# Three of the first loads asked for by ScalarE, the decay factors as a planned step, and a re-planned start

## The chip, the cores and the metric

One NeuronCore of one Trainium2 chip runs the whole kernel. The metric is the device time of one execution in microseconds; the kernel before took 299.38 us (median of three runs, 299.16 to 300.62).

## What is computed

A retention layer (attention without a softmax, with a decay by distance) feeds a feed-forward layer with an ELU. Eight batches, eight heads, 576 positions, head size 64; the feed-forward goes from 512 to 2048 and back to 512, over 8 x 576 = 4608 tokens.

```
scores = (q @ k^T) / 8                                   # per batch and head
D[i, j] = gamma_h ** (i - j)  where i >= j, else 0       # gamma_h = 1 - 2 ** (-5 - h)
x = ((scores * D) @ v)  -> [4608, 512]
h = x @ w_in                                             # [512, 2048]
g = where(h > 0, h, exp(min(h, 0)) - 1)
out = g @ w_out                                          # [2048, 512], float32
```

## The kernel before

**Tiling.** A sequence of 576 is cut in chunks of 64. The decay is split into a factor on the queries and one on the keys, `gq` and `gk` (lines 299 to 315: a table load on ScalarE and two exponentials), so that a chunk needs a triangular mask, and everything earlier goes through a running state, the sum of scaled keys times values. An *item* is one batch and 256 positions (or the last 64 of four batches, X and Y). The items of batches 0 and 1 are further cut by heads into two *units* of four heads each, numbered 0 to 7; units 0 and 1 make item 0, units 2 and 3 item 1. A unit goes through these steps: load q and k into one tile (`r`, `rqk`) and v into another, shared by the item's two units; scale the even and the odd positions of q and k by the factors (line 548, tile `st`, four halves, VectorE or GpSimd); cast v (line 558, tile `vn`); transpose q and k on TensorE (line 580) and copy them out of PSUM (line 586, tile `T`), or from unit 5 on transpose by DMA (line 569); scores and their mask (line 914, tile `pt`); its state (matmuls `f<-vn,st`), summed by VectorE (`mid`, lines 849 and 851) and cast (`s`, line 867); and the output of the unit, state part and value part, copied to `xt` (line 950).

**Feed-forward.** A block is 256 tokens (blocks 0 and 1 are items 0 and 1). `ffn1` multiplies `xt` by pieces of `w_in` into one PSUM bank at a time (`f<-xt,w_in_sb`), ScalarE and VectorE make the ELU of it (lines 1067 to 1091, tile `g`), and `ffn2` multiplies by `w_out` (`f<-w_out_sb,g`, 128x512). Block 0's `ffn1` needs the outputs of units 0 and 1 in `xt`.

**What sets the order.** Every step is an `Op` with a cost on each engine that may run it, the steps it depends on, the buffers it takes and a rank. `Plan.run` (lines 67 to 198) goes through time by these costs and gives, engine by engine, the step of lowest rank that is ready; its order is what is emitted, and each engine then runs in that order and waits on semaphores. A planned time is not seen by the chip, the order alone is. `AT` (line 227) holds a named step back to a planned time, `RANKS` (line 228) shifts its rank, `LEAD` and `ULEAD` set how far attention runs ahead of the feed-forward, `EARLY` how many units go through `early` (line 1026: scores, state and output apart) instead of `stretch` (line 998: a unit's output together with the next one's scores), and `UAPART` after which units a stretch is closed by itself. Where the plan leaves TensorE idle in the first 50 us, fillers on a zero tile are put in (lines 1213 to 1223).

**Loads.** All loads of q, k and v are issued by SyncE (line 389), chained in one order (`chain[0]`, line 412): q and k of units 0 and 1, then v of both, then units 2 and 3 alike. The weights are cast on the way by GpSimd's DMA queue, `w_in` in five pieces (line 480) and `w_out` in four (line 491). `HOLD` (line 225) puts a one-column copy on GpSimd (line 400) that reads a piece of a weight and writes the tile of a load, so that the load is asked for only when that piece has landed: unit 4's queries behind the second piece of `w_out` (`wo1`).

Of the kernel before, what the change touches and what calls it, by code (L numbers as in the profile page):

```python
# [11 lines left out]
FP32 = mybir.dt.float32  # L12
# [23 lines left out]
class Plan:  # L36
# [6 lines left out]
    def add(self, *a, **kw):  # L43
        op = Op(*a, **kw)
        self.ops.append(op)
        for key in op.use:
            self.users.setdefault(key, []).append(op)
            op.turn += self.owner.get(key, [])
        for cls, key, *_ in op.take:
            self.owner[key] = [op]  # L50
            if cls not in FREE:
                op.turn += self.takers.get(cls, [])
                self.takers[cls] = [op]
        return op
# [151 lines left out]
ISSUE = 0.65  # L206
# [2 lines left out]
TWO, STEP = 2, 4  # L209
WI, WI1, LD = 1.3, 1.65, 0.84  # L210
MOST, MOSTU = 4, 3
BD_POOL = 0.46
UB_POOL = 0.33
SCALED = 1.06
OUT = "SP"

LEAD = 128
LATE = 26.0
ULEAD = 80
UB = 2  # L220
EARLY = 6
PE_TURN = 5
APART = ()
UAPART = (7,)
HOLD = {"ldq4": "wo1"}
VLATE = (0, 1)
AT = {"wi0": 8.5, "wi1": 10.7, "wi2": 9.0, "wi3": 11.8, "wi4": 14.4, "wo0": 17.4, "wo1": 17.7, "wo2": 19.9, "wo3": 25.3, "so_0_0_0_0": 74, "so_0_1_0_0": 74, "so_1_0_0_0": 74, "so_1_1_0_0": 74, "so_2_0_0_0": 76, "so_2_1_0_0": 76, "ub2_0": 15.33, "md_4_2": 89.01, "F2_3_1_0_0": 78.57, "st2": 14.97, "g_2_6": 63.17, "cq1_0_4": 59.08, "T0_0": 4.92, "us7_1": 60.01, "F2_0_1_12_0": 46.64, "md_3_3": 66.87, "md_1_7": 35.82, "us5_0": 44.11, "ex_2_4": 55.85, "ex_2_2": 53.67, "xc1_u4": 43.93}
RANKS = {"us1_0": -2, "F1_0_1": 4, "mask0_7": 2, "g_2_1": -2, "md_3_3": 8, "A7": -4, "cv1_5": -4}
FREE = ("f", "e", "em", "g", "ot")
SURE = 3  # L230
ATT = ((0, 0), (0, 1), (1, 0), (1, 1), (2, 0), (2, 1), (3, 0), (3, 1), (4, 0), (4, 1), "X",
# [12 lines left out]
def kernel(  # L244
# [9 lines left out]
    nc = tc.nc  # L254
# [18 lines left out]
    pin = tc.keep_in_program_order  # L273
# [38 lines left out]

    (gq, gk), product, powers = decay("", pos, 4)
    product(nc.vector)
    powers()
    pos2_i = const.tile([P, 7], I32, name="pos2_i")
    pos2 = const.tile([P, 7], FP32, name="pos2")
    (gq2, gk2), product2, powers2 = decay("2", pos2, 7)
# [12 lines left out]
    plan = Plan(SLOTS)  # L331
    add = plan.add
# [4 lines left out]
    def T(cls, key, shape, dt):  # L337
        return (cls, key, shape, dt)
# [8 lines left out]
    for n, key in enumerate(ATT):  # L347
        it = Work()
# [6 lines left out]
        if not it.tail and it.b < UB:  # L355
            for w in range(2):
                u = Work()
# [25 lines left out]
    chain, holds = {}, []  # L383
# [2 lines left out]

    def load_part(name, dst, src, key, first, shape, cost=(0.9, 32)):
        def emit(op):
            pin(nc.sync.dma_start(dst(), src))  # L389

        hold = None
        if first and name in HOLD:
            behind = HOLD[name]

            def emit_h(op):
                one = tiles[key][:, 0, :1]
                if isinstance(behind, str):
                    i = int(behind[2:])
                    mark = w_in_sb[:, 0, 256 * W_IN[i][0] :] if behind[1] == "i" else w_out_sb[:, 4 * W_OUT[i][0]]
                    pin(copy[op.eng](one, mark[:, :1]))  # L400
                else:
                    pin(alu[op.eng].memset(one, 0.0))

            hold = add(f"hold{name}", {"POOL": 0.1}, [], emit_h, len(plan.ops) - 1000, take=[T("r", key, shape, FP32)])
            if isinstance(behind, str):
                holds.append((hold, behind))
            else:
                hold.early = behind
            first = False
        op = add(name, {"SP": ISSUE}, [hold], emit, len(plan.ops), take=[T("r", key, shape, FP32)] if first else [],  # L410
                 use=[] if first else [key], dma=cost, after=chain.get(0))
        if not name[3:].isdigit():
            op.most = MOST
        elif int(name[3:]) >= 5:
            op.most = MOSTU
        chain[0] = op
        return op

    def runs(src, b, hs, T):
        return src[b, hs, TB * T : TB * (T + 1), :].rearrange("h (p e) d -> p h (e d)", e=2)  # L420

    def load(it):
        n = it.n
        shape = [P, 2 * H, D]
        if it.units:
            for u, what in [(u, what) for u in it.units for what in "qkv"] if it.n not in VLATE else \
                    [(u, what) for u in it.units for what in "qk"] + [(u, "v") for u in it.units]:
                hs = slice(4 * u.w, 4 * u.w + 4)
                if what == "q":
                    u.ld = {}  # L430
                if what == "v":
                    u.ld["v"] = load_part(
                        f"ldv{u.n}", lambda hs=hs: tiles["rv", n].rearrange("p (h e) d -> p h (e d)", e=2)[:, hs],
                        runs(v, it.b, hs, it.T), ("rv", n), u.w == 0, shape, (LD, 32))
                    continue
                i = "qk".index(what)
                u.ld[what] = load_part(
                    f"ld{what}{u.n}",
                    lambda u=u, i=i: tiles["rqk", u.n].rearrange("p (h e) d -> p h (e d)", e=2)[:, 4 * i : 4 * i + 4],
                    runs((q, k)[i], it.b, hs, it.T), ("rqk", u.n), i == 0, shape, (LD if u.n or not i else 1.4, 32))  # L440
            return
        it.ld = {}
        for name, src in (("v", v), ("k", k), ("q", q)):
            key = ("r" + name, n)
            it.ld[name] = []

            def part(tag, lo, n, s, b, t, key=key, src=src, name=name):
                def dst():
                    if s is None:
                        return tiles[key][lo : lo + n].rearrange("p (h e) d -> p h (e d)", e=2)  # L450
                    return tiles[key][lo : lo + n, s * H : (s + 1) * H]

                def rows_in():
                    if s is None:
                        return src[b, :, t : t + 2 * n, :].rearrange("h (p e) d -> p h (e d)", e=2)
                    return src[b, :, t : t + n, :].rearrange("h p d -> p h d")

                it.ld[name].append(load_part(f"ld{name}{tag}_{it.n}", dst, rows_in(), key, not it.ld[name], shape,
                                             ((1.8 if s is None else KV) * n / P, 64 * n // P)))

            if not it.tail:
                t = TB * it.T
                for s in (None,) if name == "q" else range(2):
                    part("" if s is None else s, 0, P, s, it.b, t + P * (s or 0))
            elif name == "q":
                for c in range(NC):
                    part(c, c * R, R, None, it.b + c, 2 * TB)
            else:
                for s in range(2):
                    for par in range(2):  # L470
                        part(2 * s + par, par * C, C, s, it.b + 2 * s + par, 2 * TB)
# [65 lines left out]
    def prepare_unit(u):  # L537
        n = u.n
        key, vkey, tkey = ("qkn", n), ("vn", n), ("qkT", n)
        hs, begun, cq = slice(4 * u.w, 4 * u.w + 4), {}, {}  # L540
        for i in range(2):
            for e in range(2):
                g = (gq, gk)[i][:, 2 * u.T + e, hs].rearrange("p (x y) -> p x y", y=2)
                g = g.unsqueeze(3).to_broadcast([P, 2, 2, D])

                def emit(op, i=i, e=e, g=g):
                    raw = tiles["rqk", n].rearrange("p (h e) d -> p h e d", e=2)[:, 4 * i : 4 * i + 4, e]
                    pin(alu[op.eng].tensor_tensor(tiles[key][:, i, e].rearrange("p (y x) d -> p x y d", y=2),  # L548
                                                  raw.rearrange("p (x y) d -> p x y d", y=2), g, ALU.mult))

                kw, use = taking(begun, "st", key, [P, 2, 2, 4, D])
                cq[i, e] = add(f"c{'qk'[i]}{e}{n}", {"POOL": 0.62, "DVE": 0.5} if n < 4 else {"POOL": 0.64, "DVE": (0.6, 1.5)},
                               [u.ld["qk"[i]]], emit, u.rank, use=[("rqk", n), *use], **kw)
                begun.setdefault(key, cq[i, e])
        u.ck = [cq[1, 0], cq[1, 1]]

# [10 lines left out]
        if n >= PE_TURN:  # L567
            def emit_t(op):
# [3 lines left out]
                            use=[key], dma=(1.7, 64))]  # L572
            return
        u.turned = []
        for i in range(2):
            bkey = ("T", n, i)

            def emit_t(op, i=i, bkey=bkey):
                for j in range(4):
# [3 lines left out]
                    use=[key])  # L583
# [4 lines left out]
            kw, use = taking(begun, "T", tkey, [P, 8, P])  # L588
# [553 lines left out]

    for it in items:
        load(it)
    tables = late_tables()
    for it in order_of:
        (prepare_unit if it.unit else prepare_item)(it)
# [28 lines left out]
    for blk in blocks:  # L1176
        base, n = (blk.at + len(blk.its)) * 16 + 1, blk.w // P
# [20 lines left out]
    for name, shift in RANKS.items():  # L1198
        if name in named:
            named[name].rank += shift  # L1200
    order = plan.run({"PE": 1.3, "DVE": 2.2, "ACT": 3.0, "POOL": 4.4, "SP": 0.8})
    if PRINT:
        PRINT(order)
        return
# [54 lines left out]
```

## Time and profile before

| | |
|---|---|
| median of the runs | 299.38 us (299.16 to 300.62) |
| profiled execution | 299.8 us |
| its span, first to last instruction | 298.1 us |
| granted TensorE clock | 1.0 |
| TensorE busy | 288.0 us, 97% |
| VectorE, ScalarE, GpSimd busy | 66%, 56%, 40% |
| DMA | 50.67 MB, mean 170 GB/s |

How to read the rows: a timeline row is start, length in us, engine, line, operation, what is written and read, how many in a row, and in brackets how long the engine stood idle before it and what ended that. PE is TensorE, DVE VectorE, ACT ScalarE, POOL GpSimd, SPq the queue of SyncE. PE's matmuls overlap, so that the length of a group runs to the end of its last one, past the start of the next group. A row of stretches is its bounds and length, the busy time with the number of instructions, the granted clock, the DMA engines' busy share, and GB/s.

### The profile page before, as it was taken

The numbers are of one execution on the slowest core, as the hardware profiler recorded it, in microseconds if no ns is written. First come the engines' busy times: TensorE is split into PE (matmuls) and PEld (weight loads), VectorE is DVE, ScalarE is ACT, GpSimd is POOL, SyncE is SP. The second block draws the span as 40 slices with busy tenths as digits, with TensorE's granted clock in tenths as the row PEclk, the third lists the DMA queues.
The fourth block names the chain that finished last, engine by engine and source line by source line (L and its number), as shares of the span: only waits on it lengthen the run. The fifth ranks groups of instructions, "written<-read, shape, count | busy, mean of one in ns | idle before, by whom it ended". The sixth has DMA issues, their size and how long they took to land.

```text
span 298.1 us, 9218 instructions
## 1 busy us (share of the span) xinstructions
PE 288.0 (97%) x3821; PEld 188.0 (63%) x3859; DVE 196.8 (66%) x368; ACT 166.0 (56%) x306; POOL 118.2 (40%) x187
## 2 busy tenths in 40 slices
PE   6999999999999999999999999999999999999995
PEld 3778545866585857685866676767766444444444
DVE  4969633976577738878778666786786477766500
ACT  3779514855276737565656365766665568644311
POOL 5970097762536708263574462916550000000000
PEclk9999999999999999999999999999999999999999
DMA  7999999999899997989886999995761100011221
GB/s 206 286 204 207 238 272 203 256 194 243 281 189 234 195 240 206 158 227 237 196 218 143 251 215 244 177 232 128 178 107 39 73 0 35 2 36 35 50 93 70
DMA packets 128618, 50.67 MB, mean 170 GB/s; under 512 B 92608, under 2 KB 124096, under 8 KB 128576
## 3 DMA queue, kind: packets, MB, share of 16 engines
q1 hardware_dynamic: 123824, 45.89, 66.0%
q0 software_dynamic: 4752, 4.19, 8.8%
q8 instruction: 30, 0.49, 0.7%
q14 instruction: 12, 0.10, 0.1%
HBM read 36.70 MB, written 9.44 MB: 155 GB/s over the span
## 4 chain that ended last, share of the span: by engine, by line
PE 85%; DMA 8%; POOL 2%; issue 2%; SPq 1%; DVE 0%; ACT 0%; POOLq 0%; ACTq 0%
PE f L276 85%; DMA w_out_sb<-in_moe_w_out_dram 5%; DMA r<-in_q_dram 2%; DMA r<-in_v_dram 2%; POOL st L548 1%; SPq L389 1%; POOL w_in_sb L480 1%; PE f L580 0%; POOL w_out_sb L491 0%; POOL s L867 0%; POOL vn L558 0%; ACT ot L1128 0%; DVE mid L851 0%; POOL r L400 0%; DVE pt L914 0%
## 5 line engine op out<-in xcount | busy, mean ns | idle before, releaser
L276 PE MATMUL f<-xt,w_in_sb 128*128 128x256 bf16 (+1 forms) x1022 | 135.9, 286 | 0.4 <-DMA w_in_sb<-in_moe_w_in_dram 0.3
L276 PE MATMUL f<-w_out_sb,g 128*128 128x512 bf16 (+1 forms) x556 | 131.3, 373 | 3.2 <-issue 2.1
L276 PEld LDWEIGHTS <-w_in_sb 128*128 128x128 bf16 x1024 | 99.5, 98 | 33.7 <-DMA w_in_sb<-in_moe_w_in_dram 0.4
L1067 ACT ACTIVATE e<-f 128x512 f32<-128x512 f32 x144 | 85.5, 598 | 58.0 <-PE f L276 55.1
L276 PEld LDWEIGHTS <-g 128*128 128x128 bf16 x592 | 56.4, 98 | 54.8
L1081 DVE TENSOR_SCALAR em<-e 128x512 bf16<-128x512 f32 x75 | 41.2, 555 | 33.8 <-ACT e L1067 33.6
L1089 DVE SCALAR_TENSOR_TENSOR g<-e,f 128x512 bf16<-128x512 f32 x69 | 46.1, 683 | 11.6 <-ACT f L1077 10.7
L1091 DVE SCALAR_TENSOR_TENSOR g<-f,em 128x512 bf16<-128x512 f32 x75 | 50.6, 687 | 4.1 <-DVE em L1081 0.5
L605 POOL CAST kv<-r 128x512 bf16<-128x512 f32 x27 | 16.2, 613 | 56.5 <-issue 27.5
L950 ACT CAST xt<-f 128x512 bf16<-128x512 f32 (+1 forms) x37 | 21.8, 643 | 29.5 <-PE f L276 29.3
L1077 ACT ACTIVATE f<-f 128x512 f32<-128x512 f32 x64 | 37.7, 595 | 0.0
L1128 ACT COPY ot<-f 128x512 f32<-128x512 f32 (+1 forms) x37 | 21.4, 578 | 24.4 <-PE f L276 24.2
L625 POOL TENSOR_TENSOR kv<-r,gq 128x512 bf16<-128x512 f32 x28 | 30.5, 1107 | 10.4 <-DMA r<-in_q_dram 10.4
L625 POOL TENSOR_TENSOR kv<-r,gk 128x512 bf16<-128x512 f32 x28 | 29.5, 1062 | 3.8 <-DMA r<-in_k_dram 3.8
L918 DVE TENSOR_TENSOR pt<-f,mask 128x512 bf16<-128x512 f32 x28 | 18.0, 684 | 8.7 <-PE f L276 8.7
L903 POOL CAST bd<-S 128x256 bf16<-128x256 f32 x40 | 15.3, 405 | 13.0 <-DVE S L891 6.5
L891 DVE TENSOR_TENSOR S<-f,S 128x256 f32<-128x256 f32 x36 | 15.2, 422 | 7.2 <-PE f L276 4.7
L914 DVE TENSOR_TENSOR pt<-f,mask_u 128x512 bf16<-128x512 f32 x16 | 10.3, 685 | 3.0 <-PE f L276 3.0
L276 PEld LDWEIGHTS <-kv 64*64 64x64 bf16 x832 | 11.2, 104 | 0.1
L276 PE MATMUL f<-T 64*64 64x64 bf16 (+1 forms) x576 | 9.6, 199 | 0.0
L548 POOL TENSOR_TENSOR st<-r,gk 128x256 bf16<-128x256 f32 x12 | 8.0, 681 | 1.8 <-DMA r<-in_k_dram 1.8
L548 POOL TENSOR_TENSOR st<-r,gq 128x256 bf16<-128x256 f32 x10 | 6.2, 635 | 6.4 <-DMA r<-in_q_dram 6.4
(66 smaller groups left out, 128.5 us busy)
## 6 DMA issues: line engine op xcount, KB each, us to landing
r<-in_k_dram SPq DMA_DIRECT2D x32, 256.0 KB, 4.5
r<-in_v_dram SPq DMA_DIRECT2D x32, 256.0 KB, 4.7
out_dram<-ot SPq DMA_DIRECT2D x31, 256.0 KB, 2.9
r<-in_q_dram SPq DMA_DIRECT2D x12, 512.0 KB, 5.3
r<-in_q_dram SPq DMA_DIRECT2D x8, 256.0 KB, 4.4
w_out_sb<-in_moe_w_out_dram POOLq DMA_DIRECT2D x4, 512.0 KB, 14.4
w_in_sb<-in_moe_w_in_dram POOLq DMA_DIRECT2D x3, 512.0 KB, 9.7
out_dram<-ot SPq DMA_DIRECT2D x10, 128.0 KB, 2.3
```

The source lines that it names most:

```text
L276: return pin(nc.tensor.matmul(*a, **kw))
L548: pin(alu[op.eng].tensor_tensor(tiles[key][:, i, e].rearrange("p (y x) d -> p x y d", y=2), raw.rearrange("p (x y) d -> p x y d", y=2), g, ...
L605: pin(copy[op.eng](heads(tiles[nkey][:, VS[s]]), tiles["rv", n][:, s * H : (s + 1) * H]))
L625: pin(alu[op.eng].tensor_tensor(tiles[nkey][:, 2 * i + j].rearrange("p (y x d) -> p x y d", y=2, x=HP), raw.rearrange("p (x y) d -> p x y ...
L918: pin(nc.vector.tensor_tensor(pt.rearrange("p h s n -> p (h s) n"), src.rearrange("p (h n) -> p h n", n=C), mask.rearrange("p e r -> p (e ...
L950: pin(copy[op.eng](dst, src))
L1067: pin(nc.scalar.activation(tiles[ekey], tiles[hkey], AF.Exp))
L1077: pin(nc.scalar.activation(ph, ph, AF.Relu))
L1081: pin(alu[op.eng].tensor_scalar_add(em, e, -1.0))
L1089: pin(nc.vector.scalar_tensor_tensor(g, e, -1.0, ph, ALU.add, ALU.min))
L1091: pin(nc.vector.scalar_tensor_tensor(g, ph, 0.0, tiles[mkey], ALU.max, ALU.min))
L1128: pin(copy[op.eng](tiles[okey][:, :width], tiles[pkey][:, :width]))
```

## The change

Three loads, the keys of unit 0 and the values of units 0 and 1, are issued by ScalarE on its own queue and leave the chain of SyncE's loads. The two exponentials that make `gq` and `gk` become a planned step on ScalarE behind the first of these loads, and the scaling of q and k depends on it. The planner's start for ScalarE goes from 3.0 to 0.8 with it. Unit 4's queries are held behind the first piece of `w_out` instead of the second, and unit 6's behind the third (no hold before); the last piece of `w_out` is held back to a planned 34.4 instead of 25.3, and the first pieces of `w_in` move to 8.0 to 8.6. Unit 5 leaves the early ones and closes its stretch by itself; LEAD and most held times and ranks are new.

```
+ASKED = ("ldk0", "ldv0", "ldv1")
-LEAD = 128
+LEAD = 144
-EARLY = 6
+EARLY = 5
-UAPART = (7,)
-HOLD = {"ldq4": "wo1"}
+UAPART = (5, 7)
+HOLD = {"ldq4": "wo0", "ldq6": "wo2"}
...
-AT = {"wi0": 8.5, "wi1": 10.7, "wi2": 9.0, "wi3": 11.8, "wi4": 14.4, "wo0": 17.4, "wo1": 17.7, "wo2": 19.9, "wo3": 25.3,
...
+AT = {"wi0": 8.0, "wi1": 8.6, "wi2": 8.5, "wi3": 12.6, "wi4": 14.4, "wo0": 17.4, "wo1": 17.4, "wo2": 20.5, "wo3": 34.4,
...
     product(nc.vector)
-    powers()
...
-            pin(nc.sync.dma_start(dst(), src))
+            pin((nc.scalar if op.eng == "ACT" else nc.sync).dma_start(dst(), src))
...
+        own = name in ASKED
+        op = add(name, {"ACT" if own else "SP": ISSUE}, [hold], emit, -10 ** 5 if name == ASKED[0] else len(plan.ops), take=[T("r", key, shape, FP32)] if first else [],
+                 use=[] if first else [key], dma=cost, after=None if own and first else chain.get(0))
...
-        chain[0] = op
+        if not own:
+            chain[0] = op
...
-                    runs((q, k)[i], it.b, hs, it.T), ("rqk", u.n), i == 0, shape, (LD if u.n or not i else 1.4, 32))
+                    runs((q, k)[i], it.b, hs, it.T), ("rqk", u.n), i == 0, shape, (LD, 32))
...
-                               [u.ld["qk"[i]]], emit, u.rank, use=[("rqk", n), *use], **kw)
+                               [u.ld["qk"[i]], factors], emit, u.rank, use=[("rqk", n), *use], **kw)
...
+    factors = add("factors", {"ACT": 1.9}, [], lambda op: powers(pin), -10 ** 4,
+                  after=next((op for op in plan.ops if op.name in ASKED), None))
...
-    order = plan.run({"PE": 1.3, "DVE": 2.2, "ACT": 3.0, "POOL": 4.4, "SP": 0.8})
+    order = plan.run({"PE": 1.3, "DVE": 2.2, "ACT": 0.8, "POOL": 4.4, "SP": 0.8})
```

In the built program SyncE's first loads become q0, q1, k1, q2, k2, q3, k3, v2, v3, and ScalarE's stream begins with k0, the table load, `gq`, `gk`, v0, v1, the cast of v0, the copy of unit 1's transposed keys, a `mid`, the cast of v1. GpSimd scales halves of all four of the first q and k tiles, asks for three pieces of `w_in` in a row, and casts only the values of unit 3 of the first four. VectorE casts the first `s` before it scales unit 2. On TensorE the state of unit 0 stands before the scores of unit 1, and the states of units 2 and 3 stand behind the first matmuls with `w_in`.

More of the change, by code (lines that the diff above doesn't have):

```diff
@@ L220 @@
 UB = 2
-EARLY = 6
+EARLY = 5
 PE_TURN = 5
 APART = ()
-UAPART = (7,)
-HOLD = {"ldq4": "wo1"}
+UAPART = (5, 7)
+HOLD = {"ldq4": "wo0", "ldq6": "wo2"}
 VLATE = (0, 1)
-AT = {"wi0": 8.5, "wi1": 10.7, "wi2": 9.0, "wi3": 11.8, "wi4": 14.4, "wo0": 17.4, "wo1": 17.7, "wo2": 19.9, "wo3": 25.3, "so_0_0_0_0": 74, "so_0_1_0_0": 74, "so_1_0_0_0": 74, "so_1_1_0_0": 74, "so_2_0_0_0": 76, "so_2_1_0_0": 76, "ub2_0": 15.33, "md_4_2": 89.01, "F2_3_1_0_0": 78.57, "st2": 14.97, "g_2_6": 63.17, "cq1_0_4": 59.08, "T0_0": 4.92, "us7_1": 60.01, "F2_0_1_12_0": 46.64, "md_3_3": 66.87, "md_1_7": 35.82, "us5_0": 44.11, "ex_2_4": 55.85, "ex_2_2": 53.67, "xc1_u4": 43.93}
-RANKS = {"us1_0": -2, "F1_0_1": 4, "mask0_7": 2, "g_2_1": -2, "md_3_3": 8, "A7": -4, "cv1_5": -4}
+AT = {"wi0": 8.0, "wi1": 8.6, "wi2": 8.5, "wi3": 12.6, "wi4": 14.4, "wo0": 17.4, "wo1": 17.4, "wo2": 20.5, "wo3": 34.4, "so_0_0_0_0": 74, "so_0_1_0_0": 74, "so_1_0_0_0": 74, "so_1_1_0_0": 74, "so_2_0_0_0": 76, "so_2_1_0_0": 81.47, "F2_3_1_0_0": 81.39, "st2": 14.97, "g_2_6": 63.17, "cq1_0_4": 59.08, "us7_1": 60.01, "F2_0_1_12_0": 46.64, "md_3_3": 66.87, "md_1_7": 35.82, "us5_0": 44.11, "ex_2_4": 55.85, "ex_2_2": 53.67, "xc1_u4": 43.93, "ex_4_3": 87.58, "xc0_4": 82.16, "A7": 54.89, "g_1_3": 27.7, "ex_1_2": 24.95, "md_4_3": 88.96, "F1_4_0": 84.27, "bd2_3": 77.5, "cq12": 11.22, "F2_3_0_8_0": 78.02, "ex_2_0": 51.62, "ck17": 46.4, "g_6_3": 120.63, "cv7": 47.86, "cv1_4": 50.56, "us2_1": 17.29, "us0_1": 11.57}
+RANKS = {"us1_0": -2, "F1_0_1": 4, "mask0_7": 2, "g_2_1": -2, "md_3_3": 8, "A7": -4, "cv1_5": -4, "cv1_6": 4, "mask1_u6": 8, "F1_1_1": -4, "so_5_0_0_0": -8, "md_4_1": 2, "F1_1_0": 8}
 FREE = ("f", "e", "em", "g", "ot")
@@ L409, in load_part @@
             first = False
-        op = add(name, {"SP": ISSUE}, [hold], emit, len(plan.ops), take=[T("r", key, shape, FP32)] if first else [],
-                 use=[] if first else [key], dma=cost, after=chain.get(0))
+        own = name in ASKED
+        op = add(name, {"ACT" if own else "SP": ISSUE}, [hold], emit, -10 ** 5 if name == ASKED[0] else len(plan.ops), take=[T("r", key, shape, FP32)] if first else [],
+                 use=[] if first else [key], dma=cost, after=None if own and first else chain.get(0))
         if not name[3:].isdigit():
```

## The prediction

> **What bounds the kernel now.** I read the totals and the slices first, then PE's busy time by stretches, then the timeline of the head, since the change edits little else.
>
> ```profile
> span 298.1 us, 9218 instructions
> ...
> PE   6999999999999999999999999999999999999995
> ...
> 0.00:5.00 5.00, 3.74 (x21) 1.00 0.52 150
> 5.00:10.00 5.00, 4.01 (x117) 1.00 1.11 331
> 10.00:15.00 5.00, 4.81 (x105) 1.00 1.23 256
> 15.00:20.00 5.00, 4.57 (x123) 1.00 1.30 203
> ...
> 100.00:150.00 50.00, 49.26 (x773) 1.00 0.95 202
> ```
>
> PE is the bound: full in every slice but the first and last. The stretches (length, PE busy, matmuls, clock, DMA share, GB/s) put its idle time in the head: 20 - (3.74 + 4.01 + 4.81 + 4.57) = 2.87 us, of which 1.26 precede the first matmul; 1.6 are waits. In mid-kernel it idles 0.74 us in 50. Both built programs hold the same useful matmuls; only fillers differ (68 before, 64 after, the small ones on `zero`). So time can change only by when PE becomes full, and by stalls behind that.
>
> ```profile
> 15.76 1.05 PE L276 MATMUL f<-xt,w_in_sb 128*128 128x256 bf16 x8 [0.28 <-DMA w_in_sb<-in_moe_w_in_dram]
> 20.02 12.40 PE L276 MATMUL f<-xt,w_in_sb 128*128 128x256 bf16 x112
> ```
>
> The feed-forward starts at 15.76, when the first piece of w_in lands, and is unbroken from 20.02 to 32.4. Those are my two milestones. At 15.76 all four states (units 0 to 3) are done.
>
> **The change part by part.**
>
> *Factors and keys of unit 0 on ScalarE.*
>
> ```profile
> 0.80 1.28 ACT L308 ACT_TABLE_LOAD   x1 [0.80 <-PEq L1243]
> 2.10 0.32 ACT L308 ACTIVATE gq<-expo,bq 128x32 f32<-128x32 f32 x1
> 2.33 0.31 ACT L309 ACTIVATE gk<-expo,bk 128x32 f32<-128x32 f32 x1
> 3.88 0.76 DVE L548 TENSOR_TENSOR st<-r,gq 128x256 bf16<-128x256 f32 x2 [2.01 <-DMA r<-in_q_dram]
> 2.94 1.12 SPq L389 DMA_DIRECT2D r<-in_v_dram  x2
> 6.08 0.43 DVE L548 TENSOR_TENSOR st<-r,gq 128x256 bf16<-128x256 f32 x1 [0.53 <-DMA r<-in_q_dram]
> 7.63 0.62 ACT L558 CAST vn<-r 128x512 bf16<-128x512 f32 x1 [1.16 <-DMA r<-in_v_dram]
> ```
>
> ScalarE now issues k0 (0.5 us, as one of SP's two above), then loads its table, then makes gq and gk: 0.80 + 0.5 + 1.28 + 0.63 = 3.2. The first user waits for q0 until 3.88, so this costs nothing; without that cover it would cost the 0.5 us. SP's queue loses three issues ahead of unit 2, so q2, k2, q3, k3 are asked for about 1.6 us earlier.
>
> *Values of units 0 and 1 on ScalarE.* The step that decides. Each load signals one of eight completion semaphores, taken in turn; a load that takes one in use waits, on its issuing engine, for the older load to land. In the built program the turn is k0, q0, q1, k1, q2, k2, q3, k3, v2, v3, v0, v1. So v0 waits on ScalarE for q1 to land, and v1 for k1. Before, v0 was fifth and waited for nothing: asked for at 2.94, in use at 7.63 (4.7 us). q1 lands by 6.08, so v0 is asked for at about 6.1. How long it then takes no row shows for a second hardware queue:
>
> ```profile
> DMA to landing us min/median/max: 3.0/4.5/6.3
> 4.50:5.00 0.50, 0.50 (x13) 0.50 (x11) 0.50 (x2) 0.00 (x0) 0.32 (x1) 1.00 0.70 174
> 7.00:7.50 0.50, 0.46 (x12) 0.36 (x16) 0.34 (x2) 0.00 (x0) 0.50 (x1) 1.00 1.15 346
> ```
>
> The loads of the first 40 us (256 KB each) took 3.0 us at least, alone; 4.7 (v0) behind four others. At 346 GB/s one takes 0.75 us of wire. I take 3.0 plus 0.75 for sharing the wire equally with SP's queue, which still holds q3, k3, v2, v3: v0 lands at 9.85. Ends: 9.1 (no sharing) and 10.8 (the 4.7).
>
> The Trainium skill, "DMA: Bandwidth & Descriptors", section "Queues, rings and completion order", says that a DMA engine goes round-robin between queues by packet; "Issuing engines are not separate DMA queues" there adds that asking from a second engine saves only issue time. By it v0 is at the 9.85 taken above; without it at 9.1, and the sum 0.75 us less. This trace has the wire full at 346 GB/s with one queue, which agrees.
>
> Queued on ScalarE behind that cast are the copy of unit 1's transposed keys and the first `mid`; on PE, the first state stands ahead of unit 1's scores; on DVE, the cast `s` of that `mid` stands ahead of unit 2's scaling. So all three engines wait for v0. Durations:
>
> ```profile
> 5.88 0.59 ACT L586 COPY T<-f 128x512 bf16<-128x512 bf16 x1 [3.25 <-PE f L580]
> 8.75 0.27 ACT L849 COPY mid<-f 128x128 f32<-128x128 f32 x1
> 9.09 0.22 DVE L867 CAST s<-mid 128x128 bf16<-128x128 f32 x1
> 12.66 0.41 DVE L548 TENSOR_TENSOR st<-r,gq 128x256 bf16<-128x256 f32 x1
> 13.33 0.82 DVE L548 TENSOR_TENSOR st<-r,gk 128x256 bf16<-128x256 f32 x1
> 9.43 1.28 DVE L914 TENSOR_TENSOR pt<-f,mask_u 128x512 bf16<-128x512 f32 x2
> 9.22 0.28 DVE L851 TENSOR_TENSOR mid<-f,mid 128x128 f32<-128x128 f32 x1
> 14.24 0.42 DVE L586 COPY T<-f 128x512 bf16<-128x512 bf16 x1
> 20.12 0.45 DVE L950 CAST xt<-f 128x256 bf16<-128x256 f32 x1 [0.84 <-PE f L276]
> ```
>
> ScalarE: 9.85 + 0.62 (cast) + 0.59 (copy) + 0.27 (`mid`) = 11.35. DVE, in its built order: `s` 0.22, q2 0.41, masks of unit 1 1.28, k2 0.41, `mid` 0.28, q3 0.41, `mid` 0.28, k3 0.41, two copies 0.84, xt of unit 1 0.45: 5.0, so 16.4. The feed-forward needs that xt: first milestone 16.4 against 15.76, +0.65. Where a scaling runs beside GpSimd's it takes 0.82: two of them would add 0.8; I take none, since GpSimd is past most of its halves by then, and keep 0.8 for the range.
>
> *Work left at that point.* The states of units 2 and 3 now stand behind it:
>
> ```profile
> 14.89 0.59 PE L276 MATMUL f<-vn,st 64*64 64x64 bf16 x32
> ```
>
> +0.59. The second milestone is thus 1.25 late; other waste between the two (a few fillers each) is alike.
>
> *w_in earlier (due 8.0 to 8.6; GpSimd casts neither v0 nor v1).*
>
> ```profile
> 8.95 1.69 POOL L480 DMA_DIRECT2D w_in_sb<-in_moe_w_in_dram  x2
> ```
>
> The first piece is asked for about 1 us sooner than here. It was last at 15.76; the walk above is last now, so no gain. If it came no sooner, that would cost nothing either: 15.76 is before 16.4.
>
> *Unit 4's loads, w_out's end, unit 6's hold.*
>
> ```profile
> 7.04 0.40 PE L580 MATMUL f<-ident,st 128*128 128x128 bf16 x4 [0.80 <-POOL st L548]
> ...
> 37.61 0.28 PE L580 MATMUL f<-ident,st 128*128 128x128 bf16 x2
> 38.18 0.28 PE L580 MATMUL f<-ident,st 128*128 128x128 bf16 x2 [0.29 <-POOL st L548]
> 38.30 1.89 PE L276 MATMUL f<-w_out_sb,g 128*128 128x512 bf16 x8
> 46.37 0.44 PE L276 MATMUL f<-zero 128*128 128x128 bf16 x5
> ...
> 16.62 2.97 POOL L491 DMA_DIRECT2D w_out_sb<-in_moe_w_out_dram  x4
> ...
> 31.01 0.19 POOL L400 CAST r<-w_out_sb 128x1 f32<-128x1 bf16 x1 [9.43 <-DMA w_out_sb<-in_moe_w_out_dram]
> 36.94 1.19 POOL L548 TENSOR_TENSOR st<-r,gq 128x256 bf16<-128x256 f32 x2 [5.74 <-DMA r<-in_q_dram]
> DMA to landing us min/median/max: 11.7/14.4/17.4
> ```
>
> Four transposes of unit 4 spread over 0.69 us (37.61 to 38.30) for want of GpSimd's halves; 0.29 of it is idle, and four in one go end 0.40 after their start with the next work already under way: 0.4 lost. Five fillers take 0.44 to the end of the last, some 0.35 of PE's time. After, there are no fillers here, and unit 4 is asked for when the first piece of w_out lands. The four pieces, asked for from 16.6 to 18.8 (16.62 and three quarters of 2.97), land 11.7 to 17.4 us later: 28.3 to 36.2, 2.6 apart. GpSimd now passes two holds first, the second on the third piece (33.5), so it scales unit 4 from 33.5 to 35.9 (two times 1.19) instead of from 36.94. PE wants it after the late milestone and twelve 128x512 matmuls: 32.4 + 1.25 + 12 x 0.24 (1.89 for eight) = 36.5. Covered: -0.75. If the third piece slips by over 0.6 us, the gain turns into a wait. The last piece of w_out, now asked for behind that scaling (36), is first used by the 49th such matmul: 33.65 + 48 x 0.24 = 45.2, 9 us later, and w_in's first piece took 6.8 (8.95 to 15.76). Nothing.
>
> *Everything later* (LEAD, EARLY, UAPART, ranks, due times): the same matmuls on a full PE; between 0.3 less and 0.3 more idle time, I take 0.
>
> **Sum:** +0.65 + 0.59 - 0.75 = +0.5. The profiled execution took 299.8 (span 298.1 and 1.7 around it), 0.4 above the median of the runs, 299.38. On the median: **299.9**, own range 299.2 to 300.8.
>
> **The rivals.**
>
> *Slower: v0 lands at 10.8.* Place: ScalarE's cast of v0, with three engines behind. Price: 0.95 for the landing and 0.4 for one slow scaling, so 299.9 + 1.35, 301.3. It decides against me once v0 lands after about 10.6 (or the feed-forward starts after 17.5). For it: the 4.7 us of before's own v0, and SP's four loads in flight. Against: nothing stands ahead of v0 on its own queue.
>
> *A little faster: the dip closes.* With k0 on another queue, the wire might not fall to 174 GB/s at 4.5; q1 would land about 0.7 sooner and v0 with little sharing, at 8.4. The walk then gives 15.0, so w_in bounds again, just under 15: -0.75 + 0.6 - 0.75 = -0.9, 298.5. Against: nothing in the rows ties the dip to k0.
>
> *Clearly faster: the change does what it says*, the wait behind q1 costing nothing. All 1.6 us of waits in the head and the 0.75 go: 299.4 - 2.35 = 297.0. Against: the waits are in the built program.
>
> *Slower: the clock.*
>
> ```profile
> 1.26 3.17 PE L276 MATMUL f<-zero 128*128 128x512 bf16 x7 [1.26 <-DVE zero L281]
> ```
>
> The first seven 128x512 take 0.45 us each against 0.24 later, though the profile's clock column says 1.00: PE starts at half speed. A wait of 0.80 (at 7.04) did not bring that back; the wait for v0 (about 8.5 to 10.5) is 2 us. If it did, 3.2 us at half speed on the feed-forward would cost 1.6: 301.5. The Trainium skill, "TensorE: Matmul & The Clock Gate", section "Part 1: The HAM clock gate (the "warmup" mystery)", puts the return at an idle window of about 3.4 us; by it 2 us is too short, and the sum stays. No row shows a wait that long.
>
> **How the numbers follow.** Forecast 0.43; v0 at 10.8 0.27; dip closed 0.13; as it says 0.11; clock 0.06. Within 0.5% (1.5 us, about what a measurement of this kernel can tell from no change) are the forecast and the closed dip: 0.56. Faster 0.11, slower 0.27 + 0.06 = 0.33. The range covers the forecast, the closed dip, v0's ends and the slow scalings: 297.9 to 301.6; the clearly faster case is left out.
>
> **What would show it.** ScalarE's issue of v0 starts when q1 lands (5.3 to 6.1), not at 3.2; the cast of v0 waits on its load and starts near 9.9; DVE's `s` near 11.4; the first w_in matmul near 16.4 and not released by w_in; the long run of w_in matmuls ends near 33.6; unit 4's transposes without a gap. I am wrong if v0 is cast before 8.5, or if GpSimd's second hold ends after 35.

## The result and the profile after

The changed kernel takes **302.62 us** (median of six runs, 301.06 to 303.15), the kernel before 299.56 us (six runs, 298.85 to 300.62): ratio 1.0096, 95% interval 1.0072 to 1.0120. It is slower, by 3.1 us where +0.5 us was forecast, and 1.0 us beyond the range.

The page of after first: the span, PE in slices, the granted clock in slices.

```profile
span 299.3 us, 9239 instructions
...
PE   7699999999999999999999999999999999999995
...
PEclk9799999999999999999999999999999999999999
```

The loss is in the head again, but there is a new line in it: the second slice of the clock reads 7. Before it read 9 everywhere. Next the timeline of after, where the walk of the prediction can be followed.

```profile
4.22 1.03 PE L1224 MATMUL f<-ident,zero 128*128 128x128 bf16 x10
5.08 0.68 PE L582 MATMUL f<-ident,st 128*128 128x128 bf16 x4
5.50 1.28 ACTq L389 DMA_DIRECT2D r<-in_v_dram  x2
10.22 0.62 ACT L560 CAST vn<-r 128x512 bf16<-128x512 f32 x1 [7.06 <-DMA r<-in_v_dram]
10.88 0.32 PE L277 MATMUL f<-vn,st 64*64 64x64 bf16 x16 [2.65 <-ACT vn L560]
11.54 0.54 DVE L869 CAST s<-mid 128x128 bf16<-128x128 f32 x1 [2.22 <-ACT mid L851]
13.89 1.85 PE L1224 MATMUL f<-ident,zero 128*128 128x128 bf16 x20
18.18 1.04 PE L277 MATMUL f<-xt,w_in_sb 128*128 128x256 bf16 x8
24.54 10.65 PE L277 MATMUL f<-xt,w_in_sb 128*128 128x256 bf16 x96
35.03 2.75 PE L277 MATMUL f<-w_out_sb,g 128*128 128x512 bf16 x12
```

ScalarE asks for v0 at 5.50, casts it at 10.22, and PE (2.65 us) and VectorE (2.22 us) stand behind it. So far this is the forecast (6.1, near 9.9, near 11.4). Then it parts: the first w_in matmul starts at 18.18 and not at 16.4, the long run of them ends at 35.19 (24.54 + 10.65) and not at 33.65. Between lies the row at 13.89: 20 fillers in 1.85 us. In the stretches of after (columns as before, with every engine's busy time) the clock of that time can be read:

```profile
11.00:12.00 1.00, 1.00 (x39) 0.86 (x34) 0.46 (x2) 0.50 (x2) 0.62 (x2) 0.84 1.28 292
12.00:15.00 3.00, 3.00 (x61) 2.57 (x53) 3.00 (x8) 2.29 (x6) 0.92 (x2) 0.50 1.41 200
15.00:16.00 1.00, 1.00 (x20) 1.00 (x18) 0.44 (x2) 0.38 (x3) 0.98 (x3) 0.95 1.23 212
```

A mean of 0.84 in the twelfth microsecond is 0.32 us at half speed, 0.95 in the sixteenth is 0.1 us: TensorE ran at half speed from 11.68 to 15.1, 3.4 us. The mean clock of this execution is 0.993, and its time, 301.06 us, is the shortest of the six. The next has 0.993 too (301.77 us); the other four have 0.988 to 0.989 and take 302.53 to 303.15 us, which fits half speed for about twice as long (0.5 x 6.8 of 301 us is 0.0113).

Behind the head time comes back. The span is 1.2 us longer, though w_out's first matmul is 2.78 us late (35.03 against the 32.25 of before's timeline): 1.6 us, twice what was forecast. GpSimd's holds and unit 4's transposes in after:

```profile
28.56 0.18 POOL L400 CAST r<-w_out_sb 128x1 f32<-128x1 bf16 x1 [3.19 <-DMA w_out_sb<-in_moe_w_out_dram]
33.94 0.19 POOL L400 CAST r<-w_out_sb 128x1 f32<-128x1 bf16 x1 [5.19 <-DMA w_out_sb<-in_moe_w_out_dram]
34.60 1.18 POOL L550 TENSOR_TENSOR st<-r,gq 128x256 bf16<-128x256 f32 x2 [0.47 <-DMA r<-in_q_dram]
37.62 0.39 PE L582 MATMUL f<-ident,st 128*128 128x128 bf16 x4
38.71 0.39 PE L582 MATMUL f<-ident,st 128*128 128x128 bf16 x4
```

The second hold ends at 34.1 (forecast 33.5) and the transposes run without a gap.

### The profile page after: what moved, and what is told of

It reads as the page before. It is cut to its first block, busy times and chain, and to the rows that moved or that the text cites. A ratio compares the mean times of both kernels' runs of the same rounds, so it can differ in the third digit from the quotient of the medians.

```text
span 299.3 us, 9239 instructions
## 1 busy us (share of the span) xinstructions
PE 291.3 (97%) x3855; PEld 188.8 (63%) x3855; DVE 195.4 (65%) x371; ACT 163.6 (55%) x301; POOL 119.3 (40%) x190
## 4 chain that ended last, share of the span: by engine, by line
PE 95%; DMA 3%; ACT 0%; SPq 0%; issue 0%; ACTq 0%
PE f L277 94%; DMA r<-in_v_dram 2%; DMA r<-in_q_dram 1%; PE f L1224 1%; PE f L582 0%; ACT vn L560 0%; SPq L389 0%; ACT ot L1130 0%; ACTq L1130 0%
## 5 line engine op out<-in xcount | busy, mean ns | idle before, releaser
L277 PE MATMUL f<-w_out_sb,g 128*128 128x512 bf16 (+1 forms) x592 | 138.4, 374 | 0.0
L1083 DVE TENSOR_SCALAR em<-e 128x512 bf16<-128x512 f32 x81 | 39.9, 494 | 38.1 <-ACT e L1069 38.0
L1093 DVE SCALAR_TENSOR_TENSOR g<-f,em 128x512 bf16<-128x512 f32 x81 | 54.7, 687 | 4.1
L1091 DVE SCALAR_TENSOR_TENSOR g<-e,f 128x512 bf16<-128x512 f32 x63 | 42.4, 682 | 11.6 <-ACT f L1079 10.7
L607 POOL CAST kv<-r 128x512 bf16<-128x512 f32 x28 | 16.9, 619 | 57.8 <-issue 30.6
L1079 ACT ACTIVATE f<-f 128x512 f32<-128x512 f32 x59 | 34.7, 594 | 0.0
L277 PEld LDWEIGHTS <-kv 64*64 64x64 bf16 x832 | 10.8, 104 | 0.0
L550 POOL TENSOR_TENSOR st<-r,gq 128x256 bf16<-128x256 f32 x12 | 7.5, 644 | 3.1 <-DMA r<-in_q_dram 2.2
L277 PEld LDWEIGHTS <-T 64*64 64x64 bf16 x576 | 7.5, 109 | 1.6 <-issue 0.8
```

What stands on the lines that cost most here:

```text
L277: return pin(nc.tensor.matmul(*a, **kw))
L607: pin(copy[op.eng](heads(tiles[nkey][:, VS[s]]), tiles["rv", n][:, s * H : (s + 1) * H]))
L1079: pin(nc.scalar.activation(ph, ph, AF.Relu))
L1083: pin(alu[op.eng].tensor_scalar_add(em, e, -1.0))
L1091: pin(nc.vector.scalar_tensor_tensor(g, e, -1.0, ph, ALU.add, ALU.min))
L1093: pin(nc.vector.scalar_tensor_tensor(g, ph, 0.0, tiles[mkey], ALU.max, ALU.min))
```

## The experiments

Theory after the result: v0's wait for q1 makes the head late, and TensorE's idle time in that wait brings half speed back, a cost of its own. Rivals: the second queue itself is the cost (sharing the wire), or the re-planned order is worse by itself. All medians stand against runs of before on the same chip: 299.43 us for E1 to E4, 299.24 us on another chip for E5 to E7. In the table the first three columns are of the profiled execution; all but the ratio are in us.

| | first w_in matmul | first w_out matmul | span | median | ratio to before, 95% interval |
|---|---|---|---|---|---|
| before | 15.76 | 32.25 | 298.1 | 299.43, 299.24 | |
| after | 18.18 | 35.03 | 299.3 | 302.62 | 1.0096 (1.0072 to 1.0120) |
| E1 values before the table load | 14.95 | 32.12 | 296.6 | 298.24 | 0.9959 (0.9946 to 0.9973) |
| E2 values on SyncE | 15.56 | 32.42 | 296.7 | 298.40 | 0.9973 (0.9956 to 0.9990) |
| E3 44 fillers in the wait | 16.89 | 33.74 | 299.9 | 301.42 | 1.0069 (1.0042 to 1.0096) |
| E4 before with late values | 21.50 | 37.84 | 302.9 | 305.35 | 1.0194 (1.0176 to 1.0212) |
| E5 before with early values | 15.57 | 32.34 | 297.5 | 298.91 | 0.9990 (0.9980 to 1.0001) |
| E6 E1 with the old hold | 14.57 | 31.86 | 296.5 | 298.24 | 0.9966 (0.9953 to 0.9979) |
| E7 eight fillers in the wait | 19.43 | 36.29 | 301.0 | 302.77 | 1.0122 (1.0102 to 1.0143) |

**E1: the changed kernel, v0 and v1 asked for ahead of ScalarE's table load.** They get the second and third of the semaphore turn and wait for nothing; no other engine's order differs.

```
+    vals = [op for op in order if op.name in ASKED[1:]]
+    order = [op for op in order if op not in vals]
+    at = order.index(next(op for op in order if op.name == ASKED[0])) + 1
+    order[at:at] = vals
```

> The changed kernel with one step moved: ScalarE asks for v0 and v1 right behind k0, ahead of the table load and the factors, so that their turn of the completion semaphores is still free; the order on the other engines is that of the changed kernel. If the wait behind q1 is the cause: v0 lands near 7.0 instead of 10.19, TensorE's idle 2.65 us and the half clock of 11.7 to 15.1 go, the first w_in matmul comes at 15.7 or before (18.18 in the changed kernel), and the time is 298 to 299.6. If the re-planned order itself loses (states behind the first w_in matmuls, held times, ranks): 301.5 to 303. If two hardware queues sharing the wire is what makes v0 late: v0 and v1 are still on ScalarE's queue, v0 lands after 8.5, 301 to 302.6.

The timeline of E1:

```profile
1.32 1.16 ACTq L389 DMA_DIRECT2D r<-in_v_dram  x2
4.68 0.37 SPq L389 DMA_DIRECT2D r<-in_q_dram  x1
6.21 0.62 ACT L560 CAST vn<-r 128x512 bf16<-128x512 f32 x1 [1.87 <-DMA r<-in_v_dram]
14.95 1.04 PE L277 MATMUL f<-xt,w_in_sb 128*128 128x256 bf16 x8
34.71 0.39 PE L582 MATMUL f<-ident,st 128*128 128x128 bf16 x4
```

The cast stands at 6.21, the head is back (32.12), the clock is 1.0 throughout, and 4.4 us are gone in the median: E1 is faster than both kernels. So neither ScalarE's queue nor the re-planned order costs anything; the place of v0 behind q1 does. The turn of semaphores shows in the second row: SyncE asks for q3 only at 4.68, when k0 has landed, and that costs nothing here.

**E2: the changed kernel, v0 and v1 asked for by SyncE behind k1**, k0 left on ScalarE.

```
...
+    at = order.index(next(op for op in order if op.name == "ldk1")) + 1
+    order[at:at] = vals
+    for op in vals:
+        op.eng = "SP"
```

> The changed kernel with v0 and v1 asked for by SyncE again, behind k1; k0 and everything else as changed. If the wait is the cause: v0 lands near 7.5, no half clock, 298 to 299.6, like the run with the values ahead of the table. If the sharing of two queues is the cause: this one is at 299 and that one above 301. If the re-planned order loses: both stay above 301.5.

```profile
7.18 0.62 ACT L560 CAST vn<-r 128x512 bf16<-128x512 f32 x1 [4.02 <-DMA r<-in_v_dram]
13.13 0.62 ACT L560 CAST vn<-r 128x512 bf16<-128x512 f32 x1 [2.39 <-DMA r<-in_v_dram]
14.00 0.24 PE L277 MATMUL f<-T,s 64*64 64x128 bf16 x2 [1.58 <-ACT s L869]
15.56 1.04 PE L277 MATMUL f<-xt,w_in_sb 128*128 128x256 bf16 x8
```

One microsecond later at the cast than E1, equal at the end (298.40): whose queue it is matters little. The values of unit 2 are now late instead (cast at 13.13, with ScalarE's cast `s` behind it) and PE idles 1.58 us at 12.4 to 14.0; the clock of this execution stays at 1.00 behind that gap. One of E2's twelve runs took 300.75 us at a mean clock of 0.994, the others 297.99 to 299.01 us at 0.998 to 1.0: that fits one stretch of 3.4 us at half speed (0.5 x 3.4 of 299 us is 0.0057). No trace of that run shows where it lay.

**E3: the changed kernel with 44 zero matmuls ahead of unit 0's state**, so that the wait stays and TensorE does not idle in it.

```
+            if op.name == "st0":
+                bank = next(tiles[key] for key in op.use if isinstance(key[0], tuple))
+                for _ in range(44):
+                    mm(bank[:, :P], zero[:, :P], zero[:, :P], start=True, stop=True)
```

> The changed kernel with 44 matmuls of 128x128 on zeros (0.056 us each, 2.5 us) put into TensorE's wait in front of the first state; the loads and the wait behind q1 stay. If the clock is a cause of its own: it stays at 1.0, the walk from v0's landing gives a first w_in matmul at 16.4 to 16.8 instead of 18.18, and the time is 300 to 301 (302.6 less one or two stretches of 3.4 us at half speed). If the clock is only a sign: no gain, 302 to 303.

The timeline, and then two stretches (clock, DMA share and GB/s stand last in a row):

```profile
8.14 2.62 PE L277 MATMUL f<-zero 128*128 128x128 bf16 x44
10.84 0.32 PE L277 MATMUL f<-vn,st 64*64 64x64 bf16 x16
13.03 1.29 PE L1224 MATMUL f<-ident,zero 128*128 128x128 bf16 x20
16.89 1.04 PE L277 MATMUL f<-xt,w_in_sb 128*128 128x256 bf16 x8
48.78 0.42 PE L277 MATMUL f<-T 64*64 64x128 bf16 x16 [1.53 <-DMA T<-st]
```

```profile
8.00:11.00 3.00, 2.92 (x66) 2.84 (x63) 1.25 (x3) 0.83 (x2) 2.44 (x4) 1.00 1.15 346
11.00:16.00 5.00, 5.00 (x134) 4.27 (x125) 4.51 (x11) 3.57 (x11) 2.56 (x5) 1.00 1.35 220
```

The state still starts at 10.84, but there is no half speed: the same 20 fillers take 1.29 us instead of 1.85, the first w_in matmul comes 1.29 us sooner, and so does w_out's (33.74 against 35.03). That is the price of one stretch of half speed; what is left, 1.49 us against before, is the wait alone. In the median E3 gains 1.2 us on the changed kernel; it was expected at 300 to 301 us, and the intervals of the two ratios overlap, so that the traces and not the medians show the gain. E3's runs, all at a clock of 0.998 to 1.0, spread from 300.17 to 302.89 us. Its profiled execution gives its gain back at 48.78, where PE waits 1.53 us for unit 5's transpose by DMA; why that lands later there is not settled.

**E4: the kernel before, v0 and v1 asked for by ScalarE and behind v3 in the semaphore turn**, so that they wait for q1 and k1; the other engines' order is that of before.

```
-            pin(nc.sync.dma_start(dst(), src))
+            pin((nc.scalar if name in ("ldv0", "ldv1") else nc.sync).dma_start(dst(), src))
...
+    names = ("ldq2", "ldk2", "ldq3", "ldk3", "ldv2", "ldv3", "ldv0", "ldv1")
+    moved = [next(op for op in order if op.name == name) for name in names]
...
```

> The kernel before with one part of the change alone: v0 and v1 asked for by ScalarE behind the factors, and in the turn behind v3, so that they wait for q1 and k1 as in the changed kernel; the order on the other engines is that of before. If the wait is the cause: v0 lands near 10.5, TensorE stands idle for 2 us or more, and the time is 301.5 to 303.5. If the re-planned order loses: 299 to 300, as before.

The timeline of E4, then one stretch of it:

```profile
6.17 1.21 ACTq L389 DMA_DIRECT2D r<-in_v_dram  x2
11.05 0.62 ACT L558 CAST vn<-r 128x512 bf16<-128x512 f32 x1 [3.05 <-DMA r<-in_v_dram]
11.72 0.32 PE L276 MATMUL f<-vn,st 64*64 64x64 bf16 x16 [2.58 <-ACT vn L558]
21.50 0.72 PE L276 MATMUL f<-xt,w_in_sb 128*128 128x256 bf16 x5
43.02 0.39 PE L580 MATMUL f<-ident,st 128*128 128x128 bf16 x4
```

```profile
16.00:20.00 4.00, 4.00 (x49) 0.50 1.14 163
```

The wait alone, put into the old order, costs 5.9 us in the median, beyond the 301.5 to 303.5 us expected: a later cast, 2.58 us idle and half speed to the end of that stretch at 20. Why the old order loses more by it than the new one was not taken apart. Half speed is a part of it: a mean clock of 0.988 to 0.989 in two of the five runs, the profiled one among them, fits 6.8 us, and 0.983 in the other three fits about 10 us (0.5 x 10.2 of 303 us is 0.0168). Of 5.59 us at w_out's first matmul, 0.8 are gone at the end (span +4.8): unit 4's transposes no longer wait (43.02, four in one go).

**E5: the kernel before with one part of the change**, k0, v0 and v1 asked for by ScalarE ahead of its table load.

```
+ASKED = ("ldk0", "ldv0", "ldv1")
...
-    powers()
...
-            pin(nc.sync.dma_start(dst(), src))
+            pin((nc.scalar if name in ASKED else nc.sync).dma_start(dst(), src))
+            if name == ASKED[-1]:
+                powers(pin)
...
+    moved = [next(op for op in order if op.name == name) for name in ("ldq0", *ASKED)]
+    order = moved + [op for op in order if op not in moved]
```

> The kernel before with one part of the change alone: keys of unit 0 and values of units 0 and 1 asked for by ScalarE on its own queue, ahead of its table load, none of them waiting for another load; every other engine's order is that of before. Theory (the cost is the wait behind q1, not ScalarE's queue): v0 is issued near 1.3 and lands near 6.2, the first w_in matmul starts at 15.8 or up to 0.5 us sooner (w_in's own first piece is last there, and is asked for when it was), time 298.9 to 299.8, so within 0.3% of before. Rival (asking on ScalarE's queue costs by itself, by the shared wire and the later factors): first w_in matmul after 16.5, time 300.3 or more.

```profile
15.57 1.05 PE L277 MATMUL f<-xt,w_in_sb 128*128 128x256 bf16 x8
32.34 5.34 PE L277 MATMUL f<-w_out_sb,g 128*128 128x512 bf16 x23
37.52 0.39 PE L582 MATMUL f<-ident,st 128*128 128x128 bf16 x4
```

As the theory had it: no loss, and nothing gained in the head either (32.34 against 32.25). The expectation had w_in last there; the trace shows no wait for it at 15.57. Its span is 0.6 us shorter because unit 4's transposes are in one piece.

**E6: E1 with the old hold**, unit 4 behind w_out's second piece, the last piece due at 25.3, no hold for unit 6; planned anew from there.

```
-HOLD = {"ldq4": "wo0", "ldq6": "wo2"}
+HOLD = {"ldq4": "wo1"}
...
-AT = {... "wo3": 34.4, ...
+AT = {... "wo3": 25.3, ...
```

> E1 (values ahead of the table load) with unit 4's hold and w_out's last piece put back as they were before (behind w_out's second piece, due 25.3; no hold for unit 6), planned anew from there. Theory (the hold's part is worth the 0.65 us of split transposes and the 0.37 us of fillers between 32 and 52 us): unit 4's transposes wait or split again, five fillers or so come back, time 0.8 to 1.1 above E1, 299.0 to 299.4. By the prediction's terms (0.75): 299.0. Rival (the gain of the re-planned order lies elsewhere): within 0.3 of E1, 298.0 to 298.5.

```profile
28.81 0.18 POOL L400 CAST r<-w_out_sb 128x1 f32<-128x1 bf16 x1 [6.30 <-DMA w_out_sb<-in_moe_w_out_dram]
34.76 1.18 POOL L550 TENSOR_TENSOR st<-r,gq 128x256 bf16<-128x256 f32 x2 [5.76 <-DMA r<-in_q_dram]
37.05 0.39 PE L582 MATMUL f<-ident,st 128*128 128x128 bf16 x4
```

298.24, the same as E1 (ratios 0.9966 and 0.9959, with overlapping intervals). My theory of the hold falls. With the old hold, too, GpSimd scales unit 4 at 34.76, 2.2 us sooner than before (36.94), because the earlier issues of w_in and w_out let the second piece land by 28.8 instead of 31.0. Neither split transposes nor fillers come back.

**E7: the changed kernel with eight zero matmuls in the wait** (E3's edit with 8 for 44), to shorten the idle time.

> The changed kernel with eight zero matmuls of 128x128 ahead of the first state, where the other run had 44: TensorE idles about 2.1 us there instead of 2.65. If the clock falls for an idle time of 2.1 us too: half speed from 11 to 12 on for one or two windows of 3.41 us, first w_in matmul near 18.2, time 301.0 to 302.8 as the changed kernel. If 2.1 us is too short for it: no half speed, first w_in matmul near 16.9, time 300.5 to 301.5.

The timeline, then three stretches:

```profile
10.67 0.32 PE L277 MATMUL f<-vn,st 64*64 64x64 bf16 x16 [2.20 <-ACT vn L560]
13.68 2.32 PE L1224 MATMUL f<-ident,zero 128*128 128x128 bf16 x20
15.79 0.63 PE L582 MATMUL f<-ident,st 128*128 128x128 bf16 x4
19.43 1.04 PE L277 MATMUL f<-xt,w_in_sb 128*128 128x256 bf16 x8
```

```profile
11.00:12.00 1.00, 1.00 (x24) 0.73 (x24) 0.68 (x2) 0.29 (x2) 0.83 (x2) 0.73 1.28 290
12.00:18.00 6.00, 6.00 (x85) 5.54 (x83) 3.80 (x10) 3.25 (x8) 3.50 (x6) 0.50 1.27 183
18.00:19.00 1.00, 1.00 (x34) 0.81 (x34) 0.53 (x2) 0.45 (x1) 0.00 (x0) 0.86 1.18 185
```

2.20 us of idle time bring half speed as well, here from 11.46 to 18.28, 6.8 us (read as above: 0.54 + 6 + 0.28). Its mean clock is 0.989 and it takes 302.70 us: the same mean clock as the four runs of the changed kernel from 302.53 us up. Of its other three runs two have 0.988 and 0.989, and the shortest (302.42 us) 0.992. At w_out's first matmul the second stretch of half speed costs another 1.26 us (36.29 against 35.03, though the state starts 0.2 us sooner here).

## Why the prediction was wrong

**The step that failed: the rival of the clock,** dismissed with "by it 2 us is too short, and the sum stays" and a chance of 0.06. The row at 7.04 had shown that 0.80 us does not bring half speed back; nothing had been shown for 2 us. On the chip waits of 2.20 (E7), 2.58 (E4) and 2.65 us (after) brought half speed back, in every run of these three kernels by the mean clock; the 1.58 us of E2 did not in its profiled execution, and one of its twelve runs leaves it open. The price was foreseen too small as well: 3.2 us at half speed for 1.6 us. E3 shows 1.29 us for one such stretch, and four of the six runs have two. The rule that the dismissal rested on, an idle window of about 3.4 us (the Trainium skill, "TensorE: Matmul & The Clock Gate", section "Part 1: The HAM clock gate (the "warmup" mystery)"), was the wrong guide for the onset: gaps of 2.2 us were enough. Its window length, 3413 ns, free-running, agrees with how long half speed lasted in the traces, 3.4 or 6.8 us. Neither of the two signs that I had named against me came (v0 cast before 8.5, the second hold after 35): what failed stood among the rivals, too cheap and too unlikely.

Step by step:

- *Factors and k0 on ScalarE, nothing:* held. `gk` ends at 3.16 and the first scaling waits for q0. But that scaling starts at 4.53, not 3.88: q0, asked for at the same moment as k0, came 0.65 us later than in before. This lay inside the wait for v0.
- *v0 waits for q1:* right, and shown by E1 (wait away, 4.4 us gone) and E4 (wait alone, 5.9 us). Sizes: asked for at 5.50 instead of 6.1, cast at 10.22 instead of 9.85. The load took 4.7 us with only v1 behind it on its queue, not 3.75: the estimate of equal sharing was too low, and the earlier issue hid most of it.
- *The walk to 16.4:* without the clock it is 16.89 (E3); 0.37 of the 0.5 is v0's landing.
- *States of units 2 and 3 behind it, +0.59:* the lag grows by 0.36 from the first w_in matmul (1.13) to w_out's (1.49). Together the wait cost 1.49 against 1.25.
- *Unit 4, w_out, holds, -0.75:* the sign was right, the size and the reason were not. Lateness taken back behind w_out's first matmul: 1.6 us in after, 1.4 in E1 (span -1.5, milestone -0.13). The gap in the transposes is worth about 0.65 rather than 0.4 (E5 shows a span 0.6 shorter with a milestone 0.1 later), and the rest, among it the five fillers, went with the new order. It needed no new hold (E6). What else in the order brings the last 0.4 to 0.6 us was not taken apart. It was luck that this gain came out about twice as large: it hides 0.65 to 0.85 us of the loss.
- *"In mid-kernel it idles 0.74 us in 50":* it does not. Those gaps come beside matmuls that are missing from the trace: before shows 556 matmuls with w_out, after all 592, and after idles 0.00 us from 100 to 150.
- *Against the median:* for after's own execution 1.49 + 1.29 - 1.6 gives +1.2, as its spans have it, but the 1.6 was read from those spans; with the 1.4 of E1 it is +1.4. The median lies 1.6 us above that execution. The second stretch of half speed, in four runs of six, is 1.26 of it by E7; the rest was not taken apart. I had counted on one number for all runs.

The other rivals: v0 did not land at 10.8. "The dip closes" was right in its first half (q1 let ScalarE go at 5.50, 0.6 us sooner) but not in its second. "The change does what it says", 297.0, is what E1 tries: 298.24. There the first w_in matmul comes 0.8 us sooner than before but w_out's only 0.1, since the states of units 2 and 3 stand between them now; and in the first 20 us 1.2 of the 1.6 us of waits stay (PE is busy for 17.57 us from 1.25 on).

## What to carry to other kernels

Look at what a load waits for before it is asked for: where loads share a few completion semaphores in turn, the place in the order of issues decides, and moving two loads in the order of issues is worth 4.4 us here. Price an idle time of TensorE with the half speed that may follow it (gaps from 2.2 us up did it here in every run, 1.6 us perhaps in one run of twelve), or keep it busy with zero matmuls, and read the mean clock of every run, not that of the profiled one alone. When a re-planned order comes with a change, take the two apart: here the order was a gain of about 1 us that one wait hid.

## What was not expected of the hardware

- Half speed in the middle of a busy stretch, about 0.8 us after work had resumed (idle until 10.88, half speed from 11.68; in E7 10.67 and 11.46), for 3.4 or 6.8 us in the traces.
- The changes of speed look like ticks of one steady beat. TensorE also starts at half speed, with one filler in 0.106 us (E7's 20 from 13.68 to 15.79) against 0.056 at full speed (E3's 20 from 13.03 to 14.16). So the ten fillers from 4.22 to 5.08 in after change speed near 4.85. Half speed returns 6.83 us later, at 11.68, and ends 3.4 after that; E7, worked out alike (ten fillers from 4.22 to 4.98), has 4.64, 11.46 and 18.28. By this beat of 3.41 us TensorE stood idle for 2.6 us between two ticks in after and for 2.2 in E7, while in E2 a tick near 13.0 parts the 1.58 us in 0.6 and 1.0. It would explain both the late onset and why one gap of 1.58 us might do what another does not. It fits these traces; no run moved a gap against the beat.
- Asking on a second queue did not make a load faster: v0 took 4.7 us in after (5.50 to 10.2) and 4.9 in E1 (1.32 to 6.2), as the 4.7 us of before behind four loads on one queue.
- q0 landing 0.65 us later when k0 was asked for at the same moment by another engine.
